# Splitting the context copies: 256 columns for the projection, 64 for the batched rows

## The chip, the cores and the metric

The kernel runs on one core of a Trainium2 chip. The metric is the device time of one execution in microseconds (us). Before the change the median of three runs is 849.89 us (849.73 to 851.56).

The core's engines work side by side and meet at semaphores. TensorE (PE) multiplies matrices; its weight loads are listed apart as PEld. VectorE (DVE) and ScalarE (ACT) copy and compute, and both read PSUM, where TensorE writes. GpSimd (POOL) works on SBUF. SyncE (SP) issues transfers.

## The reference

The input x has 2048 rows of 512. It is normalised, passed through a segmented attention with a recurrent memory (A), added to itself, normalised again and passed through a gated MLP with a spatial mixing matrix (B). The first part matters here:

```python
mem = mem0                                   # 8 rows of 512
for s in range(n_seg):                       # 64 segments of 32 rows
    h = concatenate([mem, xs])               # 8 + 32 = 40 rows
    q, k, v = h @ Wq, h @ Wk, h @ Wv         # 32 heads of 128
    p = softmax(mask(q @ k.T * scale))
    o = (p @ v) @ Wo                         # 40 rows of 512
    mem = o[:, :8]                           # the next segment's memory rows
    outs.append(o[:, 8:])                    # 32 rows of output
```

Segment s + 1 cannot start its projection of the memory rows before segment s has finished Wo for its first 8 rows.

## The kernel before, in words

**Batched and serial rows.** Of a segment's 40 rows, 32 go through the serial loop: the 8 of memory and the first 24 of x. The last 8 rows of x are batched: their queries, keys and values depend on x alone and are computed ahead for 16 segments at a time, and their output, which no later segment needs, is projected for four segments together. In the context buffer each group of 40 columns holds first these 8 batched rows (`M` is 8) and then the 32 serial ones.

**One segment of the loop, in the order in which TensorE takes it.** `QK` projects queries and keys (line 534), `S_half` makes scores (585, 591), `sm_sums` the sums of the exponentials (606, 611), `V_half` the values (640). Then a piece of work for later segments is put in, which comes from the list `gx` or, late in the loop, from `zcol` (four matmul steps and one copy out; for batched queries and keys the copy is `qkx_evac`, ScalarE's line 428 and VectorE's line 437). `PV_half` multiplies values with probabilities into PSUM (665, 671), which gives the context. `WoX_mm` projects a quarter of the previous four segments' batched rows (746). `Wo` projects this segment's serial rows (701), first output columns 0 to 255 into bank 6, then columns 256 to 511 into bank 0. `part_evac` (ScalarE, 713) copies each half to SBUF, `mem_out` picks out the 8 memory rows with TensorE (721) and puts them into `hT` with ScalarE (724), half by half. Then the next segment's `QK` starts.

**The context copies.** PSUM bank c (c = 0 to 3) holds eight heads' context, 8 groups of 40 columns, 320 columns in fp32. `cT_evac` scales it and copies it as bf16 to `cT`. Bank c = 0 is copied in two pieces of 160 columns by ScalarE, the first before the second `PV_half`. c = 1 is copied whole by ScalarE (line 687), c = 2 and then c = 3 whole by VectorE (line 689). `Wo` takes c in the order 0, 2, 1, 3 and reads columns 8 to 39 of each group. `cTx_copy` (GpSimd, line 709) then copies columns 0 to 7 of all 32 groups from `cT` to `cTx`, the buffer from which `WoX_mm` reads in the next four segments.

**What sets the order.** The order on each engine is the order of the calls in the program. An emitter notes which buffers each instruction reads and writes and derives the semaphore waits. A PSUM bank is one buffer for it: an instruction that reads a bank also waits for earlier readers on other engines, and one that writes it waits for all its readers. An argument `after` adds a wait by hand.

**Four segments make a row-block.** In the last one of each, VectorE also copies out the batched projection (`WoX_evac`, line 751) right after the context copies; a few segments have another copy there (`vx_evac`, line 486). After the loop, the MLP follows (lines 1166 to 1308).

Of the kernel before, what the change touches and what calls it, by code (L numbers as in the profile page):

```python
# [9 lines left out]
ACT = mybir.ActivationFunctionType  # L10
ALU = mybir.AluOpType
# [158 lines left out]
def fast_path(nc, st, keep, A_x, A_mem0, A_Wq, A_Wk, A_Wv, A_Wo, A_seg_len, B_w_in, B_w_sp, B_b_sp, B_w_out, out):  # L170
    S = A_x.shape[1]
    D = A_x.shape[2]
    H = A_Wq.shape[1]
    DH = A_Wq.shape[2]
    M = A_mem0.shape[1]
# [12 lines left out]
    scale = float(DH) ** -0.5  # L188
# [7 lines left out]
    em = Emitter(n_dma_sems=40)  # L196

    def sb(name, shape, dt):
        return st.enter_context(nc.sbuf_tensor("f_" + name, shape, dt))
# [20 lines left out]
    cTx = sb("cTx", [128, 2, H, 32], BF)  # L220
# [9 lines left out]
    cT = sb("cT", [128, 4, 320], BF)  # L230
# [32 lines left out]
    ps = st.enter_context(nc.psum_tensor("f_ps", [128, 8, 512], F32))  # L263
# [5 lines left out]
    def PB(b):  # L269
        return ("ps", b)  # L270
# [4 lines left out]
    def pe(fn, **k):  # L275
        return em.add("pe", fn, **k)

    def act(fn, **k):
        return em.add("act", fn, **k)

    def dve(fn, **k):
        return em.add("dve", fn, **k)

    def pool(fn, **k):
        return em.add("pool", fn, **k)
# [233 lines left out]
    WXB = 4  # L519
    GB = 1  # L520
    OB2 = 0
    FBK = 3
    OC = 256
# [132 lines left out]
    def pv_bank(b, c):  # L656
        return CB if (b, c) == (1, 0) else PVB[c]
# [19 lines left out]
    UNSC = math.exp(-RBIAS)  # L677


    def cT_evac(c, eng, b=None):  # L680
        bank = pv_bank(b, c)
        cols = slice(0, 320) if b is None else slice(160 * b, 160 * b + 160)
        src = ps[:, bank, cols]
        dst = cT[:, c, cols]
        tok = [("cT", c, k) for k in ((0, 1) if b is None else (b,))]
        if eng == "act":
            act(lambda e: e.activation(out=dst, in_=src, func=ACT.Copy, scale=UNSC), reads=[PB(bank)], writes=tok)  # L687
        else:
            dve(lambda e: e.tensor_scalar(out=dst, in0=src, scalar1=UNSC, scalar2=None, op0=ALU.mult),  # L689
                reads=[PB(bank)], writes=tok)  # L690

    cTh = cT[:].rearrange("p c (b g q) -> p (c b g) q", b=2, q=40)


    def Wo(cs, bank, d0, d1):
        for c in cs:
            for bg in range(8):
                b, g = bg // 4, bg % 4
                h = 16 * b + 4 * c + g
                i = 8 * c + bg  # L700
                pe(lambda e, h=h, g=g, i=i, b=b, c=c: e.matmul(  # L701
                    ps[32 * g:32 * g + 32, bank, 0:d1 - d0], lhsT=cTh[:, i, 8:40], rhs=w_o[:, h, d0:d1], start=(c == 0 and b == 0),
                    stop=(c == 3 and b == 1), tile_position=(0, 32 * g)),
                    reads=[("cT", c, b), ("Wo", h // 8)], writes=[PB(bank)])

    def cTx_copy(s):
        j = s % 4
        dst = cTx[:, (s // 4) % 2, :, 8 * j:8 * j + 8]
        pool(lambda e: e.tensor_copy(out=dst, in_=cTh[:, :, 0:8]), reads=[("cT", c, b) for c in range(4) for b in range(2)],
             writes=[("cTx", (s // 4) % 2)])  # L710

    def part_evac(s, bank, d0, d1):
        act(lambda e: e.activation(out=part[:, s % 8, d0:d1], in_=ps[:, bank, 0:d1 - d0], func=ACT.Copy), reads=[PB(bank)],  # L713
            writes=[("part", s % 8, d0 // OC)])
# [27 lines left out]
    def WoX_mm(rb, qr, bgs=range(8)):  # L742
        for bg in bgs:
            b, g = bg // 4, bg % 4
            h = 16 * b + 4 * qr + g
            pe(lambda e, h=h, g=g, i=8 * qr + bg: e.matmul(ps[32 * g:32 * g + 32, WXB, :], lhsT=cTx[:, rb % 2, i, :], rhs=w_o[:, h, :],  # L746
                                                           start=(i < 4), stop=(i >= H - 4), tile_position=(0, 32 * g)),
               reads=[("cTx", rb % 2), ("Wo", h // 8)], writes=[PB(WXB)])

    def WoX_evac(rb):  # L750
        dve(lambda e: e.tensor_copy(out=partx[:], in_=ps[:, WXB, :]), reads=[PB(WXB)], writes=["partx"])
# [223 lines left out]
    for s in range(NSEG):  # L975
        j4 = s % 4
        rb = s // 4
# [91 lines left out]
        pv = gv.pour(1) if nC(s, rb, j4) else []  # L1069
        PV_half(s, 0)  # L1070
        cT_evac(0, "act", 0)
        PV_half(s, 1)
        if not pv:
# [4 lines left out]
        if rb > 0:  # L1078
            WoX_mm(rb - 1, j4, wx)
        cT_evac(0, "act", 1)  # L1080
        cT_evac(2, "dve")
        cT_evac(1, "act")
        cT_evac(3, "dve")
        if turn:
            pv[0]("dve")
        if j4 == 3 and rb > 0:
            WoX_evac(rb - 1)
        for f in xs[4:]:
            f()
        Wo((0, 2, 1, 3), OB, 0, OC)  # L1090
        part_evac(s, OB, 0, OC)
        Wo((0, 2, 1), OB2, OC, D)
        if s + 1 < NSEG:
            mem_out(s, 0)
        Wo((3,), OB2, OC, D)
        cTx_copy(s)
        part_evac(s, OB2, OC, D)
        if j4 == 0 and rb > 0:
            F_group(rb - 1, FBK, True)
# [14 lines left out]
        if rb > 0 and len(wx) == 4:  # L1114
            WoX_mm(rb - 1, j4, range(4, 8))
# [103 lines left out]
    def zbank():  # L1219
        zcnt[0] += 1  # L1220
        return 5 + zcnt[0] % 3
# [26 lines left out]
    for i, rb in enumerate(order):  # L1248
# [3 lines left out]
        if i == 0:  # L1252
            F_group(RB - 1, XB)
            for qr in range(4):
                WoX_mm(RB - 1, qr)
            endA = em.by_eng["pe"][-1]
            WoX_evac(RB - 1)
            load_wT(1, [endA])
            sp(lambda e: e.dma_start(w_out, B_w_out.rearrange("(fb p) d -> p fb d", p=128)), writes=["w_out"], after=[endA])
# [12 lines left out]
        if i in (3, 4):  # L1272
            r, j, bank = RB - 5 + i, i % 2, zbank()
# [41 lines left out]
    for tb in range(NTB):  # L1315
        for fb in range(len(ACC) if tb == 0 else 0, FB):
            bank = 5 + fb % 3 if tb == 0 else (tb * FB + fb) % 2
# [685 lines left out]
def build_kernel(nc, A_x, A_mem0, A_Wq, A_Wk, A_Wv, A_Wo, A_seg_len, B_x, B_w_in, B_w_sp, B_b_sp, B_w_out, out):  # L2003
    args = (A_x, A_mem0, A_Wq, A_Wk, A_Wv, A_Wo, A_seg_len, B_w_in, B_w_sp, B_b_sp, B_w_out, out)
    with contextlib.ExitStack() as keep:
        with contextlib.ExitStack() as st:
            em, sems, dsems, flag = fast_path(nc, st, keep, *args)
# [88 lines left out]
```

## Time and profile before

| | |
|---|---|
| Median of 3 runs | 849.89 us (849.73 to 851.56) |
| Profiled execution | 849.45 us, of which 847.7 us from the first to the last instruction (the span) |
| Granted TensorE clock | 1.000 |
| Serial loop | 64 segments, about 10 us each, from about 52 to 690 us |
| TensorE busy | 832.2 us |
| ScalarE busy | 498.4 us |
| VectorE busy | 493.3 us |
| GpSimd busy | 154.8 us |

How to read it: in a row of the timeline stand the start in us, the duration, the engine, the line, the operation, the buffers with their shapes, and how many consecutive instructions are merged; in brackets, how long the engine had been idle and what ended that. A row of the list of waits has the waiting engine and line, what it waited for, and the total in us, the number of times and the longest. A row of a group has its count, the busy time, the mean duration in ns, and the idle time before it. Matmuls are pipelined and their ends are modelled, so a busy TensorE is not TensorE at its peak. Instructions of ScalarE and VectorE can overlap slightly with their successors in the rows. Line numbers in profiles before the change are those of the kernel before; behind the change they are higher by 2 to 13.

### The profile page before, as it was taken

To read this page: it belongs to the slowest core of one execution; us is meant where nothing else is said; L and a number is where in the kernel's file an instruction comes from. 1 tells how busy PE (TensorE), PEld (TensorE's weight loads), DVE (VectorE), ACT (ScalarE), POOL (GpSimd) and SP (SyncE) were. 2 spreads that over 40 slices of the span, in tenths; PEclk is the share of its full clock that TensorE was granted. 3 is DMA by queue.
4 is the path that set the end of the run, shared out by engine and by line. 5 is a ranking of instruction groups with operands and counts; after the bars stand their busy time and mean duration, and the time that the engine had idled before them with its cause. 6 is when DMAs were issued, how large, how long until landed. Compare 5 with 4: busy or idle time off the path is not lost.

```text
span 847.7 us, 48032 instructions
## 1 busy us (share of the span) xinstructions
PE 832.2 (98%) x22034; PEld 475.2 (56%) x22034; DVE 493.3 (58%) x1175; ACT 498.4 (59%) x1419; POOL 154.8 (18%) x409
## 2 busy tenths in 40 slices
PE   8999999999999999999999999999999999999997
PEld 8655555555555555555556556555655544444443
DVE  4446556666565656565656566566656576553443
ACT  3456677767676777667777777666666676300000
POOL 5212111112211111111222121112211123200000
PEclk9999999999999999999999999999999999999999
DMA  9972222120301130213212130523332389023101
GB/s 330 386 216 87 70 45 62 52 78 21 82 29 44 57 79 29 66 59 61 65 30 77 30 79 26 122 70 77 70 82 59 70 268 305 1 99 100 44 13 46
DMA packets 95359, 76.03 MB, mean 90 GB/s; under 512 B 46184, under 2 KB 80624, under 8 KB 95152
## 3 DMA queue, kind: packets, MB, share of 16 engines
q1 hardware_dynamic: 93232, 70.09, 28.8%
q8 instruction: 174, 2.85, 1.5%
q10 hardware_dynamic: 1648, 2.49, 0.9%
q0 software_dynamic: 272, 0.33, 0.1%
q14 instruction: 33, 0.27, 0.1%
HBM read 41.75 MB, written 20.91 MB: 74 GB/s over the span
## 4 chain that ended last, share of the span: by engine, by line
PE 93%; DMA 3%; SPq 2%; issue 1%; ACT 0%; DVE 0%; POOL 0%; POOLq 0%
PE f_ps L534 27%; PE f_ps L701 14%; PE f_ps L640 13%; PE f_ps L1206 11%; PE f_ps L422 4%; PE f_ps L746 4%; PE f_ps L1301 3%; PE f_ps L472 3%; PE f_ps L665 2%; PE f_ps L797 2%; PE f_ps L1199 2%; PE f_ps L445 2%; DMA f_arena<-in_A_Wo_dram 1%; PE f_ps L585 1%; SPq L884 1%; PE f_ps L606 1%
## 5 line engine op out<-in xcount | busy, mean ns | idle before, releaser
L534 PE MATMUL f_ps<-f_arena,f_hT 128*32 128x512 bf16 (+1 forms) x5120 | 241.3, 337 | 0.9 <-ACT f_part L713 0.5
L534 PEld LDWEIGHTS f_ps<-f_arena,f_hT 128*32 128x32 bf16 x5120 | 117.2, 96 | 99.7 <-ACT f_hT L724 34.2
L545 ACT ACTIVATE f_Tst<-f_ps 128x512 bf16<-128x512 f32 (+2 forms) x320 | 146.7, 511 | 32.8 <-PE f_ps L534 32.1
L640 PE MATMUL f_ps<-f_arena,f_hT 128*32 128x512 bf16 x2048 | 138.7, 379 | 0.0
L701 PE MATMUL f_ps<-f_arena,f_cT 128*32 128x256 bf16 x4096 | 134.6, 273 | 1.2 <-issue 0.5
L630 POOL TENSOR_TENSOR f_E_sb<-f_R_sb,f_E_sb 128x64 bf16<-128x64 f32 x128 | 47.2, 369 | 387.1 <-ACT f_R_sb L622 386.5
L701 PEld LDWEIGHTS f_ps<-f_arena,f_cT 128*32 128x32 bf16 x4096 | 95.8, 95 | 31.8 <-ACT f_cT L687 8.8
L652 DVE TENSOR_SCALAR f_V_sb<-f_ps 128x512 bf16<-128x512 f32 (+1 forms) x128 | 71.4, 558 | 54.2 <-PE f_ps L640 54.2
L1206 PE MATMUL f_ps<-f_arena 128*128 128x512 bf16 x448 | 100.6, 379 | 0.1
L553 DVE STREAM_TRANSPOSE f_QT<-f_Tst 128x256 uint32<-128x256 uint32 x128 | 57.1, 446 | 65.6 <-ACT f_Tst L545 60.9
L689 DVE TENSOR_SCALAR f_cT<-f_ps 128x320 bf16<-128x320 f32 x128 | 56.8, 486 | 40.7 <-PE f_ps L671 40.7
L713 ACT ACTIVATE f_part<-f_ps 128x256 bf16<-128x256 f32 x128 | 49.2, 384 | 41.0 <-PE f_ps L701 38.9
L1206 PEld LDWEIGHTS f_ps<-f_arena 128*128 128x128 bf16 x448 | 43.6, 98 | 52.7 <-DMA f_arena<-wT_d 0.3
L687 ACT ACTIVATE f_cT<-f_ps 128x160 bf16<-128x160 f32 (+1 forms) x192 | 53.8, 346 | 26.5 <-PE f_ps L671 26.5
L599 ACT ACTIVATE f_E_sb<-f_ps 128x224 bf16<-128x224 f32 x128 | 45.4, 355 | 39.2 <-PE f_ps L611 39.2
L553 DVE STREAM_TRANSPOSE f_KT<-f_Tst 128x256 uint32<-128x256 uint32 (+2 forms) x192 | 60.7, 342 | 5.7 <-ACT f_Tst L545 3.0
L640 PEld LDWEIGHTS f_ps<-f_arena,f_hT 128*32 128x32 bf16 x2048 | 46.0, 95 | 20.0
L724 ACT ACTIVATE f_hT<-f_ps 128x16 bf16<-128x16 f32 x126 | 23.2, 184 | 47.7 <-PE f_ps L721 47.7
L571 DVE CAST f_ps<-f_mask 128x224 f32<-128x224 bf16 x80 | 29.8, 372 | 35.3 <-ACT f_hT L402 32.4
L1212 DVE TENSOR_TENSOR f_arena<-f_ps,f_arena 128x512 f32<-128x512 f32 x28 | 19.3, 689 | 52.7 <-PE f_ps L1206 52.7
L622 ACT ACTIVATE f_R_sb<-f_R_sb 128x160 f32<-128x160 f32 x128 | 43.1, 337 | 4.4 <-ACT f_Vs L484 0.4
L746 PE MATMUL f_ps<-f_arena,f_cTx 128*32 128x512 bf16 x512 | 41.5, 383 | 0.0
(128 smaller groups left out, 1142.0 us busy)
## 6 DMA issues: line engine op xcount, KB each, us to landing
wT_d<-f_wst SPq DMA_DIRECT2D x32, 256.0 KB, 2.3
f_arena<-wT_d SPq DMA_DIRECT2D x32, 256.0 KB, 5.0
f_arena<-in_A_Wv_dram SPq DMA_DIRECT2D x4, 1024.0 KB, 13.1
f_arena<-in_A_Wk_dram SPq DMA_DIRECT2D x4, 1024.0 KB
f_arena<-in_A_Wo_dram SPq DMA_DIRECT2D x4, 1024.0 KB, 12.3
f_Vx<-vext_d SPq DMA_DIRECT2D x62, 64.0 KB
vext_d<-f_Vs SPq DMA_DIRECT2D x22, 128.0 KB, 2.7
zp_d<-f_Vs SPq DMA_DIRECT2D x20, 112.0 KB, 1.7
```

The costliest lines, as they stand in the source:

```text
L534: pe(lambda e, dc=dc, c=c, rhs=rhs: e.matmul(ps[32 * c:32 * c + 32, bank, 0:32 * nh], lhsT=hT[:, sl, dc, :], rhs=rhs, start=(dc == 0), sto ...
L545: act(lambda e: e.activation(out=st_.rearrange("p (hp i r) -> p hp i r", i=32, r=2), in_=ps[:, bank, 0:64 * np_].rearrange("p (hp r i) -> ...
L553: dve(lambda e: e.transpose(out=dst, in_=src), reads=tok, writes=[(nm, b, k) for k in halves(b, p0, np_)])
L630: pool(lambda e: e.tensor_tensor(out=ev, in0=rv, in1=ev, op=ALU.mult), reads=[("R", b), ("Ex", b)], writes=[("Ex", b)])
L640: pe(lambda e, dc=dc, c=c, c0=c0: e.matmul(ps[32 * c:32 * c + 32, bank, 0:w], lhsT=hT[:, sl, dc, :], rhs=w_v[:, dc, c0:c0 + w], start=(dc ...
L652: dve(lambda e: e.tensor_scalar(out=dst, in0=src, scalar1=VSC, scalar2=None, op0=ALU.mult), reads=[PB(bank)], writes=tok)
L687: act(lambda e: e.activation(out=dst, in_=src, func=ACT.Copy, scale=UNSC), reads=[PB(bank)], writes=tok)
L689: dve(lambda e: e.tensor_scalar(out=dst, in0=src, scalar1=UNSC, scalar2=None, op0=ALU.mult), reads=[PB(bank)], writes=tok)
L701: pe(lambda e, h=h, g=g, i=i, b=b, c=c: e.matmul(ps[32 * g:32 * g + 32, bank, 0:d1 - d0], lhsT=cTh[:, i, 8:40], rhs=w_o[:, h, d0:d1], star ...
L713: act(lambda e: e.activation(out=part[:, s % 8, d0:d1], in_=ps[:, bank, 0:d1 - d0], func=ACT.Copy), reads=[PB(bank)], writes=[("part", s % ...
L746: pe(lambda e, h=h, g=g, i=8 * qr + bg: e.matmul(ps[32 * g:32 * g + 32, WXB, :], lhsT=cTx[:, rb % 2, i, :], rhs=w_o[:, h, :], start=(i < 4 ...
L1206: pe(lambda e: e.matmul(ps[:, bank, 0:TB], lhsT=z2[:, sc, fb * 128:(fb + 1) * 128], rhs=wTb[tb % 2][:, :, sc, :], start=first, stop=last), ...
```

## The change

`cT_evac` of a whole bank (c = 1, 2, 3) now reads and writes columns 8 to 39 of each group only, 8 runs of 32, which makes 256 columns in place of 320. The two 160-column pieces of c = 0 stay as they were. `cTx_copy` is now called once per bank. For c = 2 and c = 1 ScalarE copies the 8 runs of 8 columns straight from PSUM to `cTx`, after its copy of c = 1; the first of these waits for VectorE's copy of c = 2. For c = 3 VectorE does it from PSUM, behind `WoX_evac` where there is one. For c = 0 GpSimd copies from `cT` as before, 64 columns. The last `Wo` matmul before the first `mem_out` also waits for VectorE's small copy. `WoX_mm` waits for its own bank's part of `cTx` alone.

```diff
     def cT_evac(c, eng, b=None):
         bank = pv_bank(b, c)
         cols = slice(0, 320) if b is None else slice(160 * b, 160 * b + 160)
-        src = ps[:, bank, cols]
-        dst = cT[:, c, cols]
+        src = ps[:, bank, cols].rearrange("p (i q) -> p i q", q=40)
+        dst = cT[:, c, cols].rearrange("p (i q) -> p i q", q=40)
+        if b is None:
+            src, dst = src[:, :, M:40], dst[:, :, M:40]
...
-    def Wo(cs, bank, d0, d1):
+    def Wo(cs, bank, d0, d1, after=()):
...
-                    reads=[("cT", c, b), ("Wo", h // 8)], writes=[PB(bank)])
-
-    def cTx_copy(s):
-        j = s % 4
-        dst = cTx[:, (s // 4) % 2, :, 8 * j:8 * j + 8]
-        pool(lambda e: e.tensor_copy(out=dst, in_=cTh[:, :, 0:8]), reads=[("cT", c, b) for c in range(4) for b in range(2)],
-             writes=[("cTx", (s // 4) % 2)])
+                    reads=[("cT", c, b), ("Wo", h // 8)], writes=[PB(bank)], after=after if (c, bg) == (cs[-1], 7) else ())
+
+    def cTx_copy(s, c, eng, after=()):
+        j, bank = s % 4, pv_bank(0, c)
+        dst = cTx[:, (s // 4) % 2, 8 * c:8 * c + 8, 8 * j:8 * j + 8]
+        tok = [("cTx", (s // 4) % 2, c)]
+        src = ps[:, bank, 0:320].rearrange("p (i q) -> p i q", q=40)[:, :, 0:M]
+        if eng == "act":
+            act(lambda e: e.activation(out=dst, in_=src, func=ACT.Copy, scale=UNSC), reads=[PB(bank)], writes=tok, after=after)
+        elif eng == "dve":
+            dve(lambda e: e.tensor_scalar(out=dst, in0=src, scalar1=UNSC, scalar2=None, op0=ALU.mult), reads=[PB(bank)], writes=tok)
+        else:
+            pool(lambda e: e.tensor_copy(out=dst, in_=cTh[:, 8 * c:8 * c + 8, 0:M]), reads=[("cT", c, b) for b in range(2)], writes=tok)
...
-               reads=[("cTx", rb % 2), ("Wo", h // 8)], writes=[PB(WXB)])
+               reads=[("cTx", rb % 2, qr), ("Wo", h // 8)], writes=[PB(WXB)])
...
         cT_evac(2, "dve")
         cT_evac(1, "act")
         cT_evac(3, "dve")
+        x2 = em.by_eng["dve"][-2]
+        cTx_copy(s, 2, "act", [x2])
+        cTx_copy(s, 1, "act")
         if turn:
             pv[0]("dve")
         if j4 == 3 and rb > 0:
             WoX_evac(rb - 1)
+        cTx_copy(s, 3, "dve")
+        x3 = em.by_eng["dve"][-1]
         for f in xs[4:]:
             f()
         Wo((0, 2, 1, 3), OB, 0, OC)
         part_evac(s, OB, 0, OC)
-        Wo((0, 2, 1), OB2, OC, D)
+        Wo((0, 2, 1), OB2, OC, D, [x3])
         if s + 1 < NSEG:
             mem_out(s, 0)
         Wo((3,), OB2, OC, D)
-        cTx_copy(s)
+        cTx_copy(s, 0, "pool")
         part_evac(s, OB2, OC, D)
```

## The prediction

> **What bounds the kernel now.** I read the page first, then the chain, then the list of waits, then one segment of the timeline.
>
> ```profile
> span 847.7 us, 48032 instructions
> ...
> PE 832.2 (98%) x22034; PEld 475.2 (56%) x22034; DVE 493.3 (58%) x1175; ACT 498.4 (59%) x1419; POOL 154.8 (18%) x409
> ...
> PE 93%; DMA 3%; SPq 2%; issue 1%; ACT 0%; DVE 0%; POOL 0%; POOLq 0%
> ```
>
> TensorE carries 93% of the chain that ends last, but its 98% "busy" hides gaps: matmul ends are modelled and overlap. The weight loads (PEld) show them, because a load that waits for a semaphore stands idle openly:
>
> ```profile
> PEld f_ps L534 <- ACT f_hT L724: 34.2, 109, 0.4
> ...
> PEld f_ps L701 <- ACT f_cT L687: 8.8, 46, 0.4
> PEld f_ps L701 <- DVE f_cT L689: 8.8, 57, 0.2
> ```
>
> Line 701 is the output projection Wo, lines 687 and 689 the copies of the context from PSUM that the change edits. In 57 of the 64 segments Wo's loads are seen to wait for VectorE's copy, 8.8 us in all, 0.15 us each. Here is one of the 40 segments that hold line 428, an evacuation for keys and queries of later segments:
>
> ```profile
> 414.20 0.83 ACT L687 ACTIVATE f_cT<-f_ps 128x160 bf16<-128x160 f32 x3 [0.47 <-PE f_ps L671]
> 414.46 0.89 DVE L689 TENSOR_SCALAR f_cT<-f_ps 128x320 bf16<-128x320 f32 x2 [0.68 <-PE f_ps L671]
> 414.55 0.30 PEld L701 LDWEIGHTS f_ps<-f_arena,f_cT 128*32 128x32 bf16 x8 [0.19 <-ACT f_cT L687]
> 414.91 0.61 ACT L428 ACTIVATE f_Tst<-f_ps 128x512 bf16<-128x512 f32 x1
> 415.00 1.21 PEld L701 LDWEIGHTS f_ps<-f_arena,f_cT 128*32 128x32 bf16 x48 [0.15 <-DVE f_cT L689]
> 415.41 0.40 POOL L709 COPY f_cTx<-f_cT 128x256 bf16<-128x256 bf16 x1 [1.01 <-DVE f_cT L689]
> 415.89 0.38 ACT L713 ACTIVATE f_part<-f_ps 128x256 bf16<-128x256 f32 x1 [0.38 <-PE f_ps L701]
> 416.33 0.12 PEld L721 LDWEIGHTS f_ps<-f_G_sb,f_part 128*32 128x32 bf16 x8
> 416.62 0.18 ACT L724 ACTIVATE f_hT<-f_ps 128x16 bf16<-128x16 f32 x1 [0.34 <-PE f_ps L721]
> 416.85 0.12 PEld L534 LDWEIGHTS f_ps<-f_arena,f_hT 128*32 128x32 bf16 x8 [0.24 <-ACT f_hT L724]
> ```
>
> This is a recurrence. Wo's first half ends, ScalarE copies it (line 713, idle until Wo ends), TensorE extracts the memory rows (721), ScalarE puts them into hT (724), and the next segment's projection (534) waits for that. So what Wo gains at its start reaches the next segment whole, as long as ScalarE is free at line 713. Wo takes bank c=0 first, then c=2. Is the 0.15 us a real hole in the matmuls, or only in the loads? Narrow windows on single instructions:
>
> ```profile
> 414.68 0.39 PE L701 MATMUL f_ps<-f_arena,f_cT 128*32 128x256 bf16 x8
> 415.00 0.29 PE L701 MATMUL f_ps<-f_arena,f_cT 128*32 128x256 bf16 x4
> 414.40 0.63 ACT L687 ACTIVATE f_cT<-f_ps 128x160 bf16<-128x160 f32 x2
> 414.87 0.48 DVE L689 TENSOR_SCALAR f_cT<-f_ps 128x320 bf16<-128x320 f32 x1
> ```
>
> The eight matmuls of c=0 are two groups of four that run side by side: one group lasts 0.28, two last 0.39, so a group takes a slot of 0.11. Slots begin at 414.68 and 414.79; the third could begin at 414.90 and begins at 415.00. The hole is 0.10 us, and VectorE's first copy sets it. The wait on ScalarE at 414.55 is no hole: c=0's matmuls start when the slots before them are over.
>
> **The change part by part.** Durations come from these groups (mean ns last before the idle time):
>
> ```profile
> L687 ACT ACTIVATE f_cT<-f_ps 128x160 bf16<-128x160 f32 x128 | 32.8, 302 | 26.5 <-PE f_ps L671 26.5
> L687 ACT ACTIVATE f_cT<-f_ps 128x320 bf16<-128x320 f32 x64 | 27.8, 435 | 0.0
> L428 ACT ACTIVATE f_Tst<-f_ps 128x512 bf16<-128x512 f32 x40 | 24.3, 606 | 0.0
> L724 ACT ACTIVATE f_hT<-f_ps 128x16 bf16<-128x16 f32 x126 | 23.2, 184 | 47.7 <-PE f_ps L721 47.7
> L402 ACT ACTIVATE f_hT<-f_ps 128x384 bf16<-128x384 f32 x14 | 6.8, 488 | 0.0
> L689 DVE TENSOR_SCALAR f_cT<-f_ps 128x320 bf16<-128x320 f32 x128 | 56.8, 486 | 40.7 <-PE f_ps L671 40.7
> L652 DVE TENSOR_SCALAR f_V_sb<-f_ps 128x512 bf16<-128x512 f32 x64 | 44.3, 692 | 22.7 <-PE f_ps L640 22.7
> L652 DVE TENSOR_SCALAR f_V_sb<-f_ps 128x256 bf16<-128x256 f32 x64 | 27.2, 424 | 31.5 <-PE f_ps L640 31.5
> L463 DVE CAST f_arena<-f_ps 128x256 bf16<-128x256 f32 x24 | 10.5, 437 | 7.6 <-PE f_ps L445 6.0 <-ACT f_arena L461 1.1
> ```
>
> (1) c=2 and c=3 on VectorE, 320 to 256 columns. The same operation on 256 columns is 424 ns (line 652), so 486 - 424 = 62 ns come off. The new form is strided, 32 of every 40 columns on both sides. The nearest strided VectorE row, line 463, is 437: then 49 ns come off. The other end is 0, if the skipped columns cost as the moved ones. I take 62, since ScalarE's line 402, which reads 24 of every 32 columns, stands on the line through its dense rows (435 at 320, 606 at 512, 492 between them at 384; it is 488). The 62 is less than the hole, so it passes whole. What is late next: still c=2's copy, with 0.04 us of hole left. Then c=1 must be there two slots later (about 415.15); ScalarE's copy ends before 415.03 and gets shorter. c=3 is needed at about 415.37; its copy now ends at 414.87 + 0.48 = 415.35 and will end 0.12 earlier, both copies being shorter.
> Worth: 57 segments x 0.062 = 3.5 us; with unrecorded waits up to 63 x 0.062 = 3.9; by the strided row 57 x 0.049 = 2.8. I take 3.6.
>
> (2) c=1 on ScalarE, 320 to 256: about -50 ns of ScalarE, on no path.
>
> (3) Two 64-column copies on ScalarE (c=2, c=1), before line 428 and line 713. From 184 at 16 and 302 at 160 a 64-column copy is 184 + 48 x 0.82 = 223 ns. Neighbours overlap: two instructions of 302 and 435 span 0.63 in the row at 414.40, so 0.11 overlap, and a copy occupies about 0.115. The first of them waits for VectorE's copy of c=2 (same bank). I count from 414.46: that copy ends at +0.42, seen at +0.48 (today's ends at 414.946 and releases the load at 415.00, 0.055 later). Then two copies to +0.71, then line 428 (today at +0.45) to +1.32. Wo's end releases line 713 today at +1.43, after the change at +1.37. So the cover is the 0.38 us that ScalarE sits idle before line 713, and 0.05 of it is left, 0.16 with the overlap at line 428's end. Cost: nothing, on that cover. Without line 428 the cover is wide:
>
> ```profile
> 575.35 0.38 ACT L713 ACTIVATE f_part<-f_ps 128x256 bf16<-128x256 f32 x1 [0.87 <-PE f_ps L701]
> ```
>
> Line 428 stands in 40 segments, so 24 are free of the question. [...]
>
> (4) c=3's 64 columns on VectorE. By the slope of line 652 (268 ns for 256 columns) it takes 424 - 192 x 1.05 = 223 ns. The last Wo matmul before mem_out now waits for it; everything on TensorE's queue stands behind that one, mem_out and the next segment. The worst case is the last segment of a row-block, where line 751 goes first (in two more, line 486, as long, stands there):
>
> ```profile
> 283.07 0.89 DVE L689 TENSOR_SCALAR f_cT<-f_ps 128x320 bf16<-128x320 f32 x2 [0.69 <-PE f_ps L671]
> 283.62 1.21 PEld L701 LDWEIGHTS f_ps<-f_arena,f_cT 128*32 128x32 bf16 x48 [0.15 <-DVE f_cT L689]
> 283.88 0.68 DVE L751 CAST f_partx<-f_ps 128x512 bf16<-128x512 f32 x1
> 284.47 0.43 DVE L437 STREAM_TRANSPOSE f_arena<-f_Tst 128x256 uint32<-128x256 uint32 x1
> ```
>
> Line 751 starts at 283.88 - 0.12 and holds VectorE 0.59 (to 437's start). The copy runs from 284.35 to 284.57 and is seen at 284.63. The load that waits is the last of the 48, at 283.62 + 1.21 - 0.03 - 0.06 = 284.74. Cover 0.11; cost nothing. Line 437 behind it is pushed by at most 0.25 us, into idle time before the next segment.
>
> (5) POOL copies 64 columns of c=0 in place of 256 of all four, and waits for ScalarE alone. Nobody in this segment reads cTx; the reader is the next row-block's line 746. Nothing, either way. It now runs beside VectorE's copy of c=2, where it ran beside nothing that TensorE waits for. That pairing stands elsewhere in the trace:
>
> ```profile
> 412.88 0.31 POOL L630 TENSOR_TENSOR f_E_sb<-f_R_sb,f_E_sb 128x64 bf16<-128x64 f32 x1 [3.19 <-ACT f_R_sb L622]
> 412.88 0.43 DVE L652 TENSOR_SCALAR f_V_sb<-f_ps 128x256 bf16<-128x256 f32 x1 [0.50 <-PE f_ps L640]
> ```
>
> Line 652's 424 with POOL beside it lies 7 ns above the line through 486 at 320 and 692 at 512 (417), so I add no penalty.
>
> (6) New semaphore waits on TensorE: the first Wo matmul of the second half (bank 0, read by ScalarE's copy, over by about +0.75, needed after +1.0) and the one of (4). Both are met when reached. Nothing. No DMA is added or moved; SP's queue is as it was.
>
> Sum: 849.45 (the profiled execution, 1.75 outside its span) - 3.6 = 845.85. The median of the runs is 849.89, 0.44 higher; so 846.3.
>
> **The rivals.**
>
> A, ScalarE becomes the bound in the 40 segments with line 428 (slower). Place: line 713 starts late, and the whole recurrence with it. If the small copies do not overlap, each holds ScalarE 0.23 and line 428 ends at +0.48 + 0.46 + 0.61 = +1.55, 0.12 after today's start of line 713: 40 x 0.12 = 4.8 lost, 20 x 0.062 = 1.2 kept, 853.5. It starts to lose against today when the two copies together hold ScalarE longer than 0.37 us. For it: only 0.05 to 0.16 us of cover is left. Against it: three neighbours at 414.20 (302, 302, 435 long) span 0.83, so PSUM copies from different banks do overlap. [...]
>
> B, no gain (the change does not do what it says): the strided copies take as long as 320 columns, 486. Then nothing moves: 849.9. For it: no row has this very shape. Against it: lines 402 and 463.
>
> C, the wait of (4) shows: if the 64-column copy on VectorE took 0.4 us, 17 segments would lose about 0.07, 1.2 us: 847.5. Small, and still faster.
>
> Beside these, stalls of TensorE marked "issue" are 1% of the chain; their places may shift, about 1 us either way.
>
> **How the numbers follow.** Forecast 0.70 (845.3 to 847.2), C 0.06, B with a part-eaten gain 0.13 (848.2 to 850.3), A 0.11 (850.4 to 855). A measurement tells from no change about 0.2%, 1.7 us. Faster 0.75, same 0.13, slower 0.12. The range runs from 844.9 (3.9 us and a stall less) to 850.2, which leaves out A and little else.
>
> **What would show it.** Line 689's successor near 424 ns; Wo's 48 loads waiting 0.09 rather than 0.15; ScalarE's idle before line 713 falling from 0.38 to between 0.05 and 0.2 in segments with line 428; a segment shorter by 0.06; no wait on VectorE at the last Wo load before mem_out. The prediction is wrong if line 713 shows no idle time and starts more than 1.37 us after VectorE's first copy, or if that copy stays near 486.

## The result and the profile after

The changed kernel takes 847.48 us (median of 18 runs, 844.47 to 849.23), the kernel before, run beside it, 851.23 us (18 runs, 848.45 to 853.33). The ratio is 0.9954, 95% interval 0.9944 to 0.9964, so about 3.8 us faster where 3.6 was forecast. The profiled execution took 849.03 us and is one of the longer ones; what made parts of it long is told in the last section, and its total is not used as a measure of the change.

The page of the kernel after: span, busy time of each engine, and the shares of the chain that ended last.

```profile
span 847.3 us, 48217 instructions
...
PE 830.4 (98%) x22028; PEld 480.0 (57%) x22034; DVE 493.5 (58%) x1239; ACT 513.4 (61%) x1547; POOL 144.2 (17%) x409
...
PE 91%; SPq 5%; DMA 1%; DVE 1%; issue 1%; ACT 0%; POOL 0%; POOLq 0%
```

ScalarE is 15.0 us busier than before (513.4 against 498.4) and VectorE as busy as before (493.5 against 493.3), yet the kernel is faster: neither total says anything here, since these engines make up 0% and 1% of the chain that ended last. What does is in the list of waits of the kernel after (us in total, times, longest):

```profile
PEld f_ps L534 <- ACT f_hT L732: 34.1, 109, 0.4
...
PEld f_ps L729 <- ACT f_part L721: 18.3, 62, 0.3
...
ACT f_part L721 <- PE f_ps L703: 16.8, 28, 1.2
...
PEld f_ps L703 <- ACT f_cT L689: 9.3, 49, 0.4
```

The row in which Wo's loads (now line 703) wait for VectorE, 8.8 us and 57 times before, is gone altogether. The segment that answers to the one shown of before (timeline of the kernel after; start, duration, instruction, idle time before it), with the first copy of the next segment as the last row:

```profile
411.92 0.78 ACT L689 ACTIVATE f_cT<-f_ps 128x160 bf16<-128x160 f32 x3 [0.47 <-PE f_ps L671]
412.19 0.76 DVE L691 TENSOR_SCALAR f_cT<-f_ps 128x256 bf16<-128x256 f32 x2 [0.68 <-PE f_ps L671]
412.28 1.60 PEld L703 LDWEIGHTS f_ps<-f_arena,f_cT 128*32 128x32 bf16 x56 [0.19 <-ACT f_cT L689]
...
412.64 0.34 ACT L714 ACTIVATE f_cTx<-f_ps 128x64 bf16<-128x64 f32 x2
412.86 0.22 DVE L716 TENSOR_SCALAR f_cTx<-f_ps 128x64 bf16<-128x64 f32 x1
412.87 0.60 ACT L428 ACTIVATE f_Tst<-f_ps 128x512 bf16<-128x512 f32 x1
...
413.56 0.38 ACT L721 ACTIVATE f_part<-f_ps 128x256 bf16<-128x256 f32 x1
...
422.09 0.76 DVE L691 TENSOR_SCALAR f_cT<-f_ps 128x256 bf16<-128x256 f32 x2 [0.69 <-PE f_ps L671]
```

Count from VectorE's first copy, at 412.19. Wo's 56 loads run in one piece; before, 8 and 48 were parted by a wait of 0.15. Line 428 now starts at +0.68 and the copy that extracts the half (line 721, 713 before) at +1.37, with no idle time marked ahead of it. The next segment's first copy comes 422.09 - 412.19 = 9.90 us later. In the kernel before it came 9.97 later, at this row (the earlier one, 414.46, is in the prediction):

```profile
424.43 0.89 DVE L689 TENSOR_SCALAR f_cT<-f_ps 128x320 bf16<-128x320 f32 x2 [0.68 <-PE f_ps L671]
```

The hole itself shows in narrow windows on Wo's matmuls. Before, then after, the first twelve of them:

```profile
414.68 0.61 PE L701 MATMUL f_ps<-f_arena,f_cT 128*32 128x256 bf16 x12
```

```profile
412.41 0.55 PE L703 MATMUL f_ps<-f_arena,f_cT 128*32 128x256 bf16 x12
...
412.41 0.66 PE L703 MATMUL f_ps<-f_arena,f_cT 128*32 128x256 bf16 x16
```

Eight matmuls last 0.39 and a further group of four takes a slot of 0.11, so twelve without a hole would last 0.50. Before they last 0.61, a hole of about 0.1; after, 0.55, a hole of about 0.05. From the third group on the slots follow at 0.11 again (0.66 for sixteen).

The groups of the edited lines of the kernel after (count, busy us, mean ns, idle time before):

```profile
L691 DVE TENSOR_SCALAR f_cT<-f_ps 128x256 bf16<-128x256 f32 x128 | 48.5, 420 | 41.3 <-PE f_ps L671 41.3
...
L689 ACT ACTIVATE f_cT<-f_ps 128x256 bf16<-128x256 f32 x64 | 24.4, 382 | 0.0
...
L714 ACT ACTIVATE f_cTx<-f_ps 128x64 bf16<-128x64 f32 x128 | 21.7, 221 | 0.0
L718 POOL COPY f_cTx<-f_cT 128x64 bf16<-128x64 bf16 x64 | 15.1, 237 | 20.7 <-ACT f_cT L689 20.7
L716 DVE TENSOR_SCALAR f_cTx<-f_ps 128x64 bf16<-128x64 f32 x64 | 13.8, 215 | 0.0
```

**A measure for single parts.** Whole times of single executions scatter by 5 us, more than the change is worth. The profiles give a finer one: the distance from one segment's first VectorE copy to the next one's. Of the 63 distances, grouped by the stretch of the loop (segments 0 to 7, 8 to 40, 41 to 48, 49 to 62, which hold different inserted work), I take the lower quartile of each group as the undisturbed pitch. What the distances exceed it by, summed over the 63, I call the stalls, whatever caused them.

| Profile | Pitch, segments 8 to 40 / 41 to 48 / 49 to 62 (us) | First copy of segment 0 to that of segment 63 (us) | Sum of undisturbed pitch (us) | Stalls (us) |
|---|---|---|---|---|
| before | 9.97 / 9.80 / 9.83 | 630.70 | 624.79 | 5.9 |
| before, second profile (e10) | 9.97 / 9.80 / 9.83 | 631.05 | 624.79 | 6.3 |
| after | 9.90 / 9.74 / 9.76 | 630.06 | 620.54 | 9.5 |
| after, second profile (e9) | 9.90 / 9.74 / 9.77 | 626.70 | 620.60 | 6.1 |
| after, third profile (e11) | 9.90 / 9.74 / 9.77 | 629.63 | 620.60 | 9.0 |

The pitch is the same to 0.01 us in every profile of one kernel, and the change takes 624.79 - 620.54 = 4.3 us off its sum.

### The profile page after: what moved, and what is told of

Same layout as the page of the kernel before. It is cut to its first block, busy times and chain, and to the rows that moved or that the text cites. A ratio compares the mean times of both kernels' runs of the same rounds, so it can differ in the third digit from the quotient of the medians.

```text
span 847.3 us, 48217 instructions
## 1 busy us (share of the span) xinstructions
PE 830.4 (98%) x22028; PEld 480.0 (57%) x22034; DVE 493.5 (58%) x1239; ACT 513.4 (61%) x1547; POOL 144.2 (17%) x409
## 4 chain that ended last, share of the span: by engine, by line
PE 91%; SPq 5%; DMA 1%; DVE 1%; issue 1%; ACT 0%; POOL 0%; POOLq 0%
PE f_ps L534 27%; PE f_ps L703 14%; PE f_ps L640 13%; PE f_ps L1219 11%; PE f_ps L422 4%; PE f_ps L754 4%; PE f_ps L1314 3%; SPq L311 3%; PE f_ps L665 3%; PE f_ps L1212 2%; PE f_ps L472 2%; PE f_ps L805 2%; DMA f_arena<-in_A_Wo_dram 1%; PE f_ps L585 1%; SPq L892 1%; PE f_ps L1179 1%
## 5 line engine op out<-in xcount | busy, mean ns | idle before, releaser
L703 PE MATMUL f_ps<-f_arena,f_cT 128*32 128x256 bf16 x4096 | 130.5, 273 | 0.6 <-DMA f_arena<-in_A_Wo_dram 0.4
L703 PEld LDWEIGHTS f_ps<-f_arena,f_cT 128*32 128x32 bf16 x4096 | 98.4, 96 | 24.8 <-ACT f_cT L689 9.3
L691 DVE TENSOR_SCALAR f_cT<-f_ps 128x256 bf16<-128x256 f32 x128 | 48.5, 420 | 41.3 <-PE f_ps L671 41.3
L689 ACT ACTIVATE f_cT<-f_ps 128x160 bf16<-128x160 f32 (+1 forms) x192 | 50.5, 328 | 27.2 <-PE f_ps L671 27.2
L422 PE MATMUL f_ps<-f_arena,f_hTe 128*32 128x512 bf16 x640 | 41.9, 379 | 0.0
```

What stands on the lines that cost most here:

```text
L422: pe(lambda e, c=c, rhs=rhs: e.matmul(ps[32 * c:32 * c + 32, bank, :], lhsT=hTe[:, ck, dc, 32 * sg:32 * sg + 32], rhs=rhs, start=(dc == 0) ...
L703: pe(lambda e, h=h, g=g, i=i, b=b, c=c: e.matmul(ps[32 * g:32 * g + 32, bank, 0:d1 - d0], lhsT=cTh[:, i, 8:40], rhs=w_o[:, h, d0:d1], star ...
```

## The experiments

My theory: VectorE's copy of c = 2 alone sets the hole, its price is 62 to 66 ns a segment, and everything else in the change is covered. Rival A said that ScalarE's small copies eat the gain, rival B that the strided copy saves nothing, rival C that VectorE's small copy holds up the first extraction. Ratios below are against runs of the kernel before on the same chip.

### One copy alone, in the kernel before

```diff
     def cT_evac(c, eng, b=None):
...
+        if c == 2:
+            src, dst = (a.rearrange("p (i q) -> p i q", q=40)[:, :, M:40] for a in (src, dst))
```

> The kernel before with one access pattern altered: bank c = 2 is copied with 256 columns. Nothing else is added: GpSimd copies all batched columns from cT as before (those of c = 2 are left out and stay zero), so instruction counts and waits are those of before. Theory (the gain is this copy alone): segments follow each other at 9.90 us, and the ratio is 0.995 to 0.9965. Rival (the small copies moved off GpSimd and their earlier place matter too, as the run with only c = 2 altered, at 0.9991, might say): pitch 9.97 or ratio above 0.998.

Measured: 848.95 us, ratio 0.9969 (0.9952 to 0.9985), just above the range that was expected. The pitch is 9.90 / 9.74 / 9.76, that of the full change. The timeline of this kernel, two neighbouring segments' first copies and the loads between:

```profile
413.46 0.82 DVE L691 TENSOR_SCALAR f_cT<-f_ps 128x256 bf16<-128x256 f32 x2 [0.69 <-PE f_ps L671]
413.55 1.60 PEld L703 LDWEIGHTS f_ps<-f_arena,f_cT 128*32 128x32 bf16 x56 [0.19 <-ACT f_cT L689]
...
423.36 0.82 DVE L691 TENSOR_SCALAR f_cT<-f_ps 128x256 bf16<-128x256 f32 x2 [0.68 <-PE f_ps L671]
```

The loads run in one piece with this single edit: 423.36 - 413.46 = 9.90. So one access pattern on one of the three banks is the whole gain in pitch. Rival B falls here: with the strided copy VectorE's two copies span 0.82 where they spanned 0.89, and the pitch is shorter by the same 0.07.

### The new kernel with c = 2 alone, and with all but c = 2

The first (e1) leaves c = 1 and c = 3 whole and has GpSimd copy their batched columns from `cT`; the second (e2) leaves c = 2 whole and has GpSimd copy its batched columns:

```diff
-        if b is None:
+        if c == 2:
             src, dst = src[:, :, M:40], dst[:, :, M:40]
...
-        cTx_copy(s, 1, "act")
...
-        cTx_copy(s, 3, "dve")
-        x3 = em.by_eng["dve"][-1]
...
-        Wo((0, 2, 1), OB2, OC, D, [x3])
+        Wo((0, 2, 1), OB2, OC, D)
...
+        cTx_copy(s, 1, "pool")
+        cTx_copy(s, 3, "pool")
```

> One part alone: only bank c = 2 is copied with 256 columns (its 64 batched columns go by ScalarE from PSUM); c = 1 and c = 3 are copied whole as before, and GpSimd copies the batched columns of c = 0, 1, 3 from cT. Theory (the gain is VectorE's c = 2 copy, for which Wo's third group of matmuls waits): the whole gain of the change, 3.5 to 3.9 us below before, ratio 0.9955 to 0.996; ScalarE's last context copy before line 713 is one small copy instead of two. Rival (relief of VectorE, ScalarE or GpSimd as a whole, or c = 3's copy, brings part of it): less than half of it, ratio above 0.998.

```diff
-        if b is None:
+        if b is None and c != 2:
             src, dst = src[:, :, M:40], dst[:, :, M:40]
...
-        x2 = em.by_eng["dve"][-2]
-        cTx_copy(s, 2, "act", [x2])
...
+        cTx_copy(s, 2, "pool")
```

> The change without that part: c = 1 and c = 3 are copied with 256 columns and their batched columns by ScalarE and VectorE, c = 2 whole as before, its batched columns by GpSimd from cT. Theory: nothing, ratio 0.999 to 1.001, and Wo's loads wait 0.15 us for VectorE again. Rival (the other copies matter too): ratio below 0.998.

Measured for e1: 849.41 us, ratio 0.9991 (0.9975 to 1.0006); pitch 9.90 / 9.74 / 9.77. For e2: 851.15 us, ratio 1.0017 (1.0001 to 1.0034); pitch 9.97 / 9.80 / 9.83, that of the kernel before. The list of waits of e2:

```profile
PEld f_ps L703 <- DVE f_cT L691: 9.4, 61, 0.2
```

It has the wait on VectorE back, and e1 has no such row. The pitches part the kernels as the theory says. The totals do not: e1 was to fall by 3.5 to 3.9 us, and its median fell by 0.6 us (850.00 to 849.41), to a ratio above the 0.998 that the rival named; e2 came out a little above the 0.999 to 1.001 expected.

Part of this lies outside the span, where the pitch doesn't see it. In each of the 24 executions of e1 and e2 the time outside is 2.51 to 3.19 us, in each execution of the other kernels 1.66 to 1.85. Within the span, by the medians, e1 is 1.9 us below the kernel before (846.4 against 848.3) and e2 level with it (848.35). These two kernels have 128 and 64 more GpSimd copies than the changed one, but no run here shows that these are the cause. What makes up the rest of e1's shortfall, stalls (last section) or the scatter of the runs, isn't settled. All four kernels of this comparison (e1, e2, e3, e6) came out above the ratios expected of them; the kernel before took 850.00 us in it, and 851.23 to 851.42 in the others.

### The new kernel without the batched copies

```diff
-        x2 = em.by_eng["dve"][-2]
-        cTx_copy(s, 2, "act", [x2])
-        cTx_copy(s, 1, "act")
...
-        cTx_copy(s, 3, "dve")
-        x3 = em.by_eng["dve"][-1]
...
-        Wo((0, 2, 1), OB2, OC, D, [x3])
+        Wo((0, 2, 1), OB2, OC, D)
...
-        cTx_copy(s, 0, "pool")
```

> The changed kernel with the copies to cTx left out (the buffer is cleared once at the start, so the batched rows' output is missing) and without the wait of the last Wo matmul for VectorE. Theory (the added small copies and waits are covered): the same time as the changed kernel, ratio to before 0.9945 to 0.9965. Rival (they cost something that the gain hides): 1 to 4 us faster than the changed kernel, ratio below 0.994.

Measured: 848.56 us, ratio 0.9984 (0.9964 to 1.0003). The pitch is 9.90 / 9.74 / 9.76, as with the copies. So the 192 small copies on ScalarE and VectorE, the 64 on GpSimd and the two added waits cost nothing in pitch, and rival A is not seen. Rival C bears on the last segment of each row-block only, one in four, which a lower quartile can miss. But the median distance of just these segments (among 8 to 40) is 9.90 with the copies and without them, and no wait of Wo's loads for VectorE's small copy (line 716) stands in the lists of the three profiles of the changed kernel. Such a segment of the kernel after, the one that answers to that of step (4):

```profile
282.71 1.60 PEld L703 LDWEIGHTS f_ps<-f_arena,f_cT 128*32 128x32 bf16 x56 [0.19 <-ACT f_cT L689]
283.29 0.68 DVE L759 CAST f_partx<-f_ps 128x512 bf16<-128x512 f32 x1
283.88 0.21 DVE L716 TENSOR_SCALAR f_cTx<-f_ps 128x64 bf16<-128x64 f32 x1
```

The small copy ends at 284.09, and the loads run without a break to 284.31; the one that waits is the last of them.

The total was expected lower than it is; the profile has 10.2 us of stalls, the most of all, and the interval holds both no change and most of the expected gain, so the total decides nothing.

### How much room ScalarE has left

Two, then four more 64-column copies go to ScalarE after its own, into a buffer that nobody reads (the loop runs over 2 in e4, over 4 in e5):

```diff
         cTx_copy(s, 2, "act", [x2])
         cTx_copy(s, 1, "act")
+        for k in range(4):
+            act(lambda e, k=k: e.activation(out=scr[:, k, :, :], in_=ps[:, PVB[1], 0:320].rearrange("p (i q) -> p i q", q=40)[:, :, 0:M],
+                                            func=ACT.Copy, scale=UNSC), reads=[PB(PVB[1])])
```

> The changed kernel with two more 64-column copies on ScalarE behind the two (to a buffer that nobody reads). They end line 428 0.22 us later, at +1.51 of VectorE's first copy. Theory with overlap (the copy of line 721 may start 0.11 before line 428 ends): it starts at +1.40, 0.03 late, in 40 segments: 1 us above the changed kernel. Rival without overlap (a copy that waits for TensorE does not overlap its predecessor): +1.51 and 0.14 late, 5 to 6 us above the changed kernel, slower than before.

> The same with four more copies: line 428 ends at +1.73. With overlap the copy of line 721 starts at +1.62, 0.25 late, 10 us above the changed kernel; without, +1.73 and 14 us above. Both say that the small copies become the bound of 40 segments; if the time stays that of the changed kernel, ScalarE is not on the path at all.

Measured for e4: 848.92 us, ratio 0.9976 (0.9961 to 0.9991), 1.0 us above the changed kernel on the same chip (847.94), as expected with overlap; the sum of the pitch is 621.83, 1.3 more than in the first profile of the changed kernel. For e5: 856.78 us, ratio 1.0063 (1.0043 to 1.0082), 8.8 above, where 10 was expected; the sum is 631.26, 10.7 more. The timeline of e4 (line numbers are one higher up to 1097, the added copies):

```profile
414.21 0.76 DVE L692 TENSOR_SCALAR f_cT<-f_ps 128x256 bf16<-128x256 f32 x2 [0.69 <-PE f_ps L672]
...
414.67 0.34 ACT L715 ACTIVATE f_cTx<-f_ps 128x64 bf16<-128x64 f32 x2
414.89 0.35 ACT L1097 ACTIVATE f_scr<-f_ps 128x64 bf16<-128x64 f32 x2
415.10 0.63 ACT L429 ACTIVATE f_Tst<-f_ps 128x512 bf16<-128x512 f32 x1
415.58 0.43 ACT L722 ACTIVATE f_part<-f_ps 128x256 bf16<-128x256 f32 x1
```

and that of e5:

```profile
416.54 0.76 DVE L692 TENSOR_SCALAR f_cT<-f_ps 128x256 bf16<-128x256 f32 x2 [0.68 <-PE f_ps L672]
...
417.63 0.66 ACT L429 ACTIVATE f_Tst<-f_ps 128x512 bf16<-128x512 f32 x1
418.11 0.46 ACT L722 ACTIVATE f_part<-f_ps 128x256 bf16<-128x256 f32 x1
...
418.62 0.12 PEld L730 LDWEIGHTS f_ps<-f_G_sb,f_part 128*32 128x32 bf16 x8 [0.39 <-ACT f_part L722]
...
426.71 0.76 DVE L692 TENSOR_SCALAR f_cT<-f_ps 128x256 bf16<-128x256 f32 x2 [0.69 <-PE f_ps L672]
```

In e4 the copy of the half still starts at +1.37, but takes 0.43 in place of 0.38, as it overlaps line 429 by 0.15. A pair of small copies thus moves line 429 by 0.21 us (from +0.68 to +0.89) and the end by only 0.05. In e5 the second pair is paid in full: the copy starts at +1.57 and ends at +2.03, another 0.23, and the pitch is 426.71 - 416.54 = 10.17. In segments 49 to 62, which lack line 429, it stays at 9.77. So the cover was about two small copies wide beyond those of the change; rival A describes a real limit, and the change stays clear of it.

### A still shorter copy of c = 2

```diff
         if b is None:
             src, dst = src[:, :, M:40], dst[:, :, M:40]
+        if c == 2:
+            src, dst = src[:, :, 8:32], dst[:, :, 8:32]
```

> The changed kernel with 192 columns in place of 256 in the copy of c = 2 (the memory rows' context of this bank is left out and stays zero). Theory: the copy ends 0.06 us earlier, but only 0.04 us of the hole in front of c = 2's matmuls is left, so 57 segments gain 0.04 each, 2.3 us below the changed kernel, ratio to before 0.9925 to 0.994. Rival (the loads and not the matmuls set the pace): the whole 0.06 is gained, 3.6 us below, ratio 0.991. Other rival (the hole is closed already): no difference from the changed kernel, 0.9954.

Measured: 847.73 us, ratio 0.997 (0.9952 to 0.9988); pitch 9.85 / 9.74 / 9.74. The timeline:

```profile
411.53 0.69 DVE L693 TENSOR_SCALAR f_cT<-f_ps 128x192 bf16<-128x192 f32 x2 [0.68 <-PE f_ps L671]
```

The two copies span 0.69, 0.07 less than after the change. The pitch falls by 0.05 in segments 8 to 40, by nothing in 41 to 48 and by 0.02 to 0.03 beyond. The first twelve matmuls of Wo in this segment show that this is the rest of the hole:

```profile
411.75 0.50 PE L705 MATMUL f_ps<-f_arena,f_cT 128*32 128x256 bf16 x12
```

They take the 0.50 of three groups without a hole, after 0.61 in the kernel before and 0.55 in the changed one, so the copy is no longer what is late. The sum of the pitch is 2.4 us below that of the changed kernel, near the 2.3 expected; the ratio was expected at 0.9925 to 0.994 and did not get there. Why the middle stretch gains nothing isn't shown.

### c = 2 in two halves

```diff
-        if b is None:
+        if b is None or c == 2:
             src, dst = src[:, :, M:40], dst[:, :, M:40]
...
-        cT_evac(2, "dve")
+        cT_evac(2, "dve", 0)
+        cT_evac(2, "dve", 1)
```

> The changed kernel with the copy of c = 2 in two halves of 128 columns (4 groups each), so that Wo's first four matmuls of c = 2 wait for the first half alone. The first half ends at about +0.29 and closes the 0.04 us that are left of the hole; the second is seen at +0.56, where its matmuls need it at +0.54, and c = 3 is seen at +0.90, needed at +0.88. Theory: 0.01 to 0.02 us gained in 57 segments, about 1 us below the changed kernel before stalls; ScalarE's first small copy waits 0.08 longer, which uses up the rest of its cover in 40 segments. Rival: VectorE's extra instruction makes c = 3 late by more, pitch 9.92 or above.

Measured: 847.76 us, ratio 0.996 (0.9945 to 0.9976), with the changed kernel on the same chip at 849.87, ratio 0.9974 (0.9954 to 0.9993). The pitch is 9.86 / 9.75 / 9.75 (sum 618.76, 1.8 below the change): 0.04 less in segments 8 to 40, where 0.01 to 0.02 was expected, and 0.01 more in 41 to 48. The rival's 9.92 is not seen. So a first half that is ready earlier closes most of the rest of the hole; the intervals overlap, so it isn't shown that the kernel is faster than the changed one.

### The kernels before and after again

Unchanged copies of both, as a measure of what such comparisons can tell.

> The changed kernel unaltered, on the chip of the three runs beside it. If the gain is real and its size is set by the copy of c = 2: ratio 0.9945 to 0.9965 again, and a profile whose undisturbed segments follow each other at 9.90 us (before 9.97). What lies beyond that in single executions (TensorE's stalls marked issue) may differ by some us.

> The kernel before, unaltered, run as an experiment. Its ratio must be 1 within the interval; its profile is a second sample of TensorE's stalls at a pitch of 9.97 us (5.3 us over the undisturbed segments in the first). If closed holes let more of the stalls through, the kernels at 9.90 (8.5, 5.5, 7.9, 6.5, 9.0 us in their profiles) lie above it; if stalls fall by chance, it may lie among them.

> The changed kernel once more, beside its version in halves and on the same chip: ratio 0.9945 to 0.9965; pitch 9.90.

Measured: after, 847.94 us, ratio 0.9959 (0.9938 to 0.9981), and on a third chip 849.87 us, 0.9974 (0.9954 to 0.9993), above the 0.9945 to 0.9965 expected. The kernel before against itself: 850.11 us, 0.9986 (0.997 to 1.0003). With some ten runs a difference of 1 us, and at times 2, can't be told from none. This is why e1 and e3 are read from their pitch.

## Why the prediction was right

- **The time.** The forecast of 846.3 started from 849.89 for the kernel before. Run beside the changed kernel, that kernel took 851.23, 1.34 more. So the 847.48 lies 1.2 above the forecast, inside the whole range but outside the 845.3 to 847.2 that was given 0.70, while the difference of 3.75 is the one forecast. It also falls on the 847.5 of rival C; that this is chance is shown by e3, by the lists of waits and by the pitch.
- **The hole and who sets it.** Right. e8 gives the whole gain in pitch with one edit and e2 takes it away with one. The other parts of the change bring nothing in pitch.
- **The size of step (1).** 62 ns was taken for each copy, 66 measured (486 to 420). The strided row of line 463 (49) gave the worse figure and the dense one the better: the strided copy of 256 columns takes 420 where the dense one of line 652 takes 424, so skipped columns cost nothing here. The prediction counted 57 segments, by the waits seen; the sum of the pitch fell by 4.3, which is 63 x 0.068, so it fell in nearly all segments and the upper figure of 3.9 was the nearer one for this term.
- **The hole that remains.** 0.04 was expected, e6 finds 0.05 and the matmul rows 0.05. The forecast wait of 0.09 at the loads does not appear in the list of waits at all. The mark I had named for it was wrong, the hole it stood for was there.
- **ScalarE's cover, step (3) and rival A.** Line 428 was forecast at +0.71 and stands at +0.68; the copy of the half was forecast at +1.37 and is there. Line 428 ends at 412.87 + 0.60 = 413.47, so 0.09 is left of the cover, between the 0.05 and the 0.16 of the prediction. The overlap comes on top: in e4 the copy of the half starts 0.15 before line 429 ends, so some 0.24 was left, more than the prediction's upper figure, and e4 lost only 0.03 of pitch. Rival A's limit against the kernel before, two copies together 0.37, was also too tight: the four copies of e4 hold ScalarE from +0.46 to +0.89, and its pitch of 9.93 is still below 9.97. A 64-column copy takes 221 ns for 223 forecast. So the prediction's line through the rows of 16 columns (184) and 160 (302) holds at 64. Neighbours on ScalarE overlap by 0.10 (two of 221 span 0.34) to 0.15 (e4), where the prediction took 0.11.
- **Steps (2), (4), (5), (6).** Nothing, as forecast: e3, which leaves the batched copies out, has the pitch of the changed kernel, and no wait for the small copy of (4) is listed. VectorE's small copy takes 215 for 223.
- **What the sum left out.** It took the stalls as shifting by about 1 us either way. Over the profiles they are 2.9 us more at the new pitch than at the old one (next section), and the 4.3 us of pitch became 3.8, 3.5 and 1.4 us between the medians of the three comparisons (3.9, 3.5 and 2.2 by the ratios). That the first total came so near to 3.6 is partly luck: two small errors lean against each other, 57 segments for 63, and the stalls.

## What to carry to other kernels

A wait of a weight load is not yet a hole (here 0.15 at the loads was 0.10 in the matmuls, and a wait of 0.19 was none): look with narrow windows whether the matmuls behind it miss a slot, and a copy that sets such a hole is worth shortening by columns that the next reader doesn't need, even if they have to be copied again somewhere off the path. Before you move the rest to another engine, measure the idle time ahead of that engine's next urgent instruction and count the overlap of neighbours in it; here two more copies cost 1 us and the next two some 8. Where the change is worth less than the scatter of single executions, read the pitch of the loop, which is the same to 0.01 us in each profile.

## What was not expected of the hardware

**Stalls of TensorE.** In the loop of each profile TensorE's weight loads stand idle for 3 to 9 us in all with no semaphore behind it, marked "issue" in the rows (between 52 and 690 us 5.5 in the kernel before, 5.2 in e10, 8.7 in the kernel after, 8.4 in e11). This is most of the stalls, though not all: in the kernel before, segments 0 and 30 (counted from 0) exceed the pitch by 0.6 and 0.7 without such a mark. The stalls are also what the three profiled executions of the changed kernel differ by: 6.1, 9.0 and 9.5 us, in 845.84, 848.87 and 849.03. The longest such wait in the kernel after, between the first and the second load of the second extraction in segment 48, has a counterpart of 0.25 to 2.17 us at the same place in every other profile but that of e6 (before 1.25, e10 1.38, e11 1.48, e9 2.17). Timeline rows of the kernel after, then of the kernel before:

```profile
535.19 0.12 PEld L729 LDWEIGHTS f_ps<-f_G_sb,f_part 128*32 128x32 bf16 x7 [2.03 <-issue]
```

```profile
537.44 0.12 PEld L721 LDWEIGHTS f_ps<-f_G_sb,f_part 128*32 128x32 bf16 x7 [1.25 <-issue]
```

Summed over the loop, the excess over the pitch (e10's expectation counts it in another way and has lower figures) is 5.9, 6.3 and 4.4 us in the three profiles with the pitch of 9.97 (before twice, e2; mean 5.5), and 9.5, 6.1, 9.0, 8.7, 6.7 and 10.2 in the six with 9.90 (after three times, e8, e1, e3; mean 8.4). That the hole had been hiding short stalls, which show once it is closed, would give this, and so would the 3.4 of e5 at a pitch of 10.16 and the 6.9 and 9.3 of e6 and e7 at 9.85 and 9.86. But e10 was to lie below all the profiles at 9.90 if it is so, and its 6.3 lies above e9's 6.1. So it is argued from counts, not shown, and what causes the stalls stays open.

**The clock after a stall.** In the first profile of the changed kernel that stall is followed by a drop of the granted clock. Windows of the kernel after (us; PE, PEld, DVE, ACT and POOL busy; granted clock; DMA share; GB/s), then of the kernel before, then of the changed kernel's second profile (e9):

```profile
533.20:535.20 2.00, 0.08 (x9) 0.01 (x4) 0.66 (x2) 0.00 (x0) 0.00 (x0) 1.00 0.19 66
535.20:538.80 3.60, 3.60 (x43) 1.56 (x47) 0.59 (x2) 1.63 (x4) 0.00 (x0) 0.53 0.58 117
538.80:542.00 3.20, 3.20 (x131) 2.19 (x123) 2.17 (x6) 2.05 (x7) 0.00 (x0) 1.00 0.39 120
```

```profile
536.20:537.50 1.30, 0.15 (x13) 0.06 (x12) 0.69 (x2) 0.00 (x0) 0.00 (x0) 1.00 0.03 4
537.50:541.00 3.50, 3.50 (x107) 2.07 (x111) 1.64 (x5) 2.61 (x7) 0.00 (x0) 1.00 0.57 85
```

```profile
531.85:534.00 2.15, 0.08 (x6) 0.01 (x2) 0.68 (x2) 0.00 (x0) 0.00 (x0) 1.00 0.21 65
534.00:537.50 3.50, 3.50 (x107) 2.06 (x111) 1.59 (x5) 2.56 (x7) 0.00 (x0) 1.00 0.74 116
```

After 2.0 us with almost no matmul the clock stood at 0.53 for 3.6 us; after 1.25 us it stayed at 1.00. But in e9, the same kernel, the stall at this place was longer, 2.17 us, and the clock stayed at 1.00 behind it. So the length of the stall alone does not decide, and what does stays open. With the drop, the segment took 13.5 us, 3.8 over the pitch, of which 2.0 is the stall; in the kernel before it took 11.1, 1.3 over, and in e9 12.0, 2.25 over. The remaining 1.7 us or so are about what the profiled execution lies above the median (849.03 against 847.48), but executions without such a drop reach 849 too (e11: 848.87).
